# Attention and two feed-forward layers in one kernel: normalising twelve score tiles inside the product that turns them

## The chip, the cores and the metric

The kernel runs on one core of one Trainium2 chip. The metric is device time in microseconds (us), the median of several runs. A core has TensorE (PE, matrix products into PSUM; PEld is its weight load), VectorE (DVE), ScalarE (ACT), GpSimd (POOL) and SyncE (SP), each with its own in-order instruction queue. In the profile TensorE's clock is granted at one of two levels, 2.4 GHz (shown as 1.00) and 1.2 GHz (0.50).

## The reference, cut to what matters

```
q_rot, k_rot = rotate(q), rotate(k)                 # rotary embedding; q, k, v: (4, 8, 576, 64) float32
scores = q_rot @ k_rot.T / sqrt(64)
attn = exp(scores - max(scores))
attn = attn / (sum(attn) + 1e-09)                   # the step that the change moves
x = (attn @ v) as (2304, 512)
h = max(x @ w1, x @ w2, x @ w3)                     # 512 -> 768
y = h @ w_out                                       # 768 -> 512
g = y @ w_in; out = (g * sigmoid(g)) @ w_out2       # 512 -> 2048 -> 512
```

## The kernel before, in words

The attention works on 80 tiles, 20 for each of the 4 batches. A tile (b, hp, t) holds 128 query rows of the pair of heads hp, so its scores are two blocks of 128 x 576; the tile with t = 4 holds the last 64 queries of both heads on 128 partitions and has one block of 576. The list `tiles` takes, for each batch, first t = 0 and 1 of the four pairs and then t = 2, 3, 4 of the four pairs. Here tiles are counted from 0 in that order: tile 10 is the first with t = 4, and tiles[0:12] is tiles 0 to 11, all of batch 0.

Step j of `attention` (L625) does this for the tiles around j. `tile_scores` (L425) makes the scores of tile j on TensorE in float32 (L437 and L440, for t = 4 L430 and L431); there is one score buffer in PSUM. `tile_max` (L446) takes the row maximum on VectorE (L450) and the exponentials and their sums on ScalarE (L457, two instructions, one for each head). `tile_norm` (L463) runs for tile j-1: it adds 1e-9 to the sums on ScalarE (L466), takes the reciprocal on VectorE (L467), and scales the 128 x 576 exponentials of each head in place on ScalarE (L469). `tile_turn` (L532) runs for tile j-2 in batch 0: it transposes the tile in 9 pieces of 128 x 128 on TensorE (L551, three pieces for one PSUM buffer "tr", of which there are two) and copies each three out to the buffer `pt`, on ScalarE (L555) or VectorE (L557). A running count `evacs` chooses which: of the first 27 copies every third is on ScalarE, and later two of three (L554). A tile with t = 4 has six pieces (L540, L475, L476) and copies of its own. `av` (L559) then multiplies `pt` with v (L571, L575). The later batches turn their tiles by DMA and VectorE (`tile_move`, `tile_flip`) and are not touched.

Between these steps runs other work of the first 130 us. `qk_rope` and `qk_turn` (L387, L393, L399, L401 to L410) prepare q and k; GpSimd does most of the rotation. `prep_w1` loads the twelve pieces of w1, w2 and w3 as float64 and narrows each one: ScalarE L229, GpSimd L233 (for two pieces ScalarE L235), VectorE L248 and L249, a maximum on ScalarE (L155), and later a split in two float16 halves by GpSimd L175 and VectorE L178. From tile 8 on `moe1` (L674) adds groups of 12 or more float16 products (L670) for the first feed-forward layer, so many by a budget (`pace`, `RATE`), and these go on until the end of the kernel.

The order in which instructions stand in each engine's queue is made at build time by a scheduler; `tc.issue_after` pins a few of them. `z_p` is a ring of four 128 x 256 buffers, otherwise used when the second layer's weights are narrowed, which begins after step 20.

Of the kernel before, what the change touches and what calls it, by code (L numbers as in the profile page):

```python
# [17 lines left out]
P = 128  # L18
# [4 lines left out]
def fused_kernel(  # L23
# [439 lines left out]
    def tile_norm(key):  # L463
        e, m = e_t[key], heads(key)
        r = small.tile([P, 2], F32, tag="rec", name="rec")
        nc.scalar.activation(out=r[:, 0:m], in_=sum_t.pop(key)[:, 0:m], func=AF.Copy, bias=1e-9)  # L466
        nc.vector.reciprocal(out=r[:, 0:m], in_=r[:, 0:m])  # L467
        for g in range(m):
            nc.scalar.activation(out=e[:, HK[g]], in_=e[:, HK[g]], func=AF.Copy, scale=r[:, g:g + 1])  # L469

    def turn_last(e, to):

        tr = ps_t.tile([P, 512], F32, tag="tr", name="tr")
        with tc.issue_after(last["score"]):
            nc.tensor.transpose(tr[:, 0:P], e[:, 448:576], ident)  # L475
            nc.tensor.transpose(tr[0:64, P:2 * P], e[:, 512:576], ident)  # L476
        to = to.rearrange("p (i q) -> p i q", i=2)
# [54 lines left out]
    def tile_turn(key):  # L532
        b, hp, t = key
        n = P
        e = e_t.pop(key)
        pt, o = pt_of(key)
        if t == 4:
            tr = ps_t.tile([P, 512], F32, tag="tr", name="tr")
            for c in range(4):
                nc.tensor.transpose(tr[:, c * P:(c + 1) * P], e[:, c * P:(c + 1) * P], ident)  # L540
            t4 = tr.rearrange("p (c q i g) -> p g c i q", c=4, g=2, i=2)
            to = [pt[:, c:c + 4, o:o + 64].rearrange("p c (i q) -> p c i q", i=2) for c in (0, 5)]
            nc.scalar.activation(out=to[0], in_=t4[:, 0], func=AF.Copy)
            nc.vector.tensor_copy(out=to[1], in_=t4[:, 1])
            turn_last(e, pt[:, 4, o:o + 64])
            return
        for j in range(3):
            tr = ps_t.tile([P, 512], F32, tag="tr", name="tr")
            for i in range(3):
                c = 3 * j + i  # L550
                nc.tensor.transpose(tr[:, i * n:(i + 1) * n], e[0:n, c * P:(c + 1) * P], ident[0:n, 0:n])  # L551
            to, of = pt[:, 3 * j:3 * j + 3, o:o + n], tr[:, 0:3 * n].rearrange("p (a n) -> p a n", a=3)
            evacs[0] += 1
            if evacs[0] % 3 == 1 if evacs[0] < 28 else evacs[0] % 3:  # L554
                nc.scalar.activation(out=to, in_=of, func=AF.Copy)  # L555
# [65 lines left out]

    LOOSE = 25
    LAST = [(B - 1, hp, t) for hp in range(NP) for t in PARTS[1][2]]

# [821 lines left out]
```

## Time and profile before

| | us |
|---|---|
| median of 3 runs | 976.12 (973.97 to 977.35) |
| the profiled execution | 973.05, of which the span is 971.3 |
| TensorE busy in the span | 902.0 (93%) |
| VectorE, ScalarE, GpSimd busy | 710.9, 603.9, 442.3 |

The span runs from the first instruction to the last; 1.75 us lie around it. The page lists busy times of each engine over the span and groups of instructions by source line; the trace can be asked for any stretch of it. A row of a timeline gives the start, the length, the engine, the line, the operation and how many instructions it merges; an idle time before it stands in brackets with what ended it. Rows of TensorE overlap, since a product begins before the one ahead has ended: what one costs in a stream is the distance between two starts.

### The profile page before, as it was taken

Reading aid. Unit: us, or ns where it says so; the run is one execution under the profiler, and the core shown is the slowest. Engines: PE = TensorE matmul, PEld = TensorE weight load, DVE = VectorE, ACT = ScalarE, POOL = GpSimd, SP = SyncE. Lnnn points to the kernel's source line nnn. Section 1 sums busy time; section 2 is a strip of 40 time slices with the busy share of each in tenths; the row PEclk is TensorE's granted clock in tenths of the full one; section 3 lists DMA queues with packets and bytes.
Section 4 is the critical chain, followed back from the end, with each engine's and each line's share of the span. In section 5 each row is a group of like instructions: output and inputs, shape, how many; then the busy total and the mean of one; then the engine's idle time right before and its main releaser. Section 6 shows DMA issues by size and latency. Waiting matters only on the chain.

```text
span 971.3 us, 19058 instructions
## 1 busy us (share of the span) xinstructions
PE 902.0 (93%) x6802; PEld 667.4 (69%) x6802; DVE 710.9 (73%) x1295; ACT 603.9 (62%) x1381; POOL 442.3 (46%) x482
## 2 busy tenths in 40 slices
PE   2787898899999899999998999999998999999997
PEld 1454665566655566566654687788887888888886
DVE  6779888867789576898887667465787866856654
ACT  1987587757687666798877535363555545544442
POOL 6745584960325400421211047264486467365363
PEclk9788999999999999999999999999999999999999
DMA  6943034958888984899989763164553434324101
GB/s 153 295 135 108 17 109 125 185 108 187 196 184 192 202 153 87 229 237 244 264 234 208 175 206 126 51 210 130 162 167 99 134 122 136 123 91 136 61 1 44
DMA packets 185198, 146.29 MB, mean 151 GB/s; under 512 B 51216, under 2 KB 168720, under 8 KB 185104
## 3 DMA queue, kind: packets, MB, share of 16 engines
q1 hardware_dynamic: 183600, 144.36, 57.9%
q8 instruction: 54, 0.88, 0.4%
q10 hardware_dynamic: 1504, 0.72, 0.3%
q14 instruction: 40, 0.33, 0.1%
HBM read 90.51 MB, written 26.21 MB: 120 GB/s over the span
## 4 chain that ended last, share of the span: by engine, by line
PE 54%; DMA 10%; DVE 7%; ACT 6%; SPq 4%; issue 3%; POOL 2%; DVEq 0%; ACTq 0%; POOLq 0%
PE m L670 11%; PE m L1102 8%; PE mb L1102 6%; DMA pt<-e 4%; PE c L1165 4%; PE a L1165 4%; PE b L1165 4%; PE xp L575 3%; PE mg L670 3%; PE s L440 3%; ACT e L457 2%; PE d L1165 2%; SPq L508 2%; DMA w8s<-w8scr 2%; POOL gsum L1049 1%
## 5 line engine op out<-in xcount | busy, mean ns | idle before, releaser
L670 PEld LDWEIGHTS <-w 128*128 128x128 f16 x1632 | 160.3, 99 | 62.2 <-issue 18.1
L670 PE MATMUL m<-x,w 128*128 128x256 f16 (+1 forms) x1356 | 188.6, 289 | 10.7 <-DVE t L689 5.1
L1165 PEld LDWEIGHTS <-g 128*128 128x128 f16 x1485 | 145.2, 98 | 16.9
L1102 PEld LDWEIGHTS <-w8s 128*128 128x128 f16 x1344 | 131.0, 98 | 16.1 <-issue 0.9
L450 DVE TENSOR_REDUCE nb<-s 128x2 f32<-128x1152 f32 (+1 forms) x80 | 98.5, 1232 | 37.2 <-PE s L440 30.0
L457 ACT ACTIVATE e<-s,nb 128x576 f32<-128x576 f32 x144 | 105.1, 734 | 28.6 <-DVE nb L450 26.1
L469 ACT ACTIVATE e<-e,rec 128x576 f32<-128x576 f32 x144 | 104.0, 766 | 11.2 <-DVE rec L467 10.4
L366 POOL TENSOR_TENSOR w<-qk,sin_sb 128x512 f32<-128x512 f32 (+2 forms) x40 | 42.8, 1072 | 122.7 <-DMA qk<-in_q_dram 93.5
L575 PE MATMUL xp<-pt,vd 128*64 128x256 f32 (+1 forms) x512 | 79.0, 422 | 0.9 <-DVE pt L530 0.9
L440 PE MATMUL s<-T 64*128 64x512 f32 x256 | 78.7, 685 | 0.0
L970 POOL TENSOR_TENSOR zs<-za 128x128 f32<-128x128 f32 x32 | 16.5, 527 | 129.8 <-DMA za<-zwi 68.3
L530 DVE STREAM_TRANSPOSE pt<-pt 128x1024 f32<-128x1024 f32 (+1 forms) x60 | 67.6, 1127 | 9.4 <-DMA pt<-e 9.4
L1054 DVE SCALAR_TENSOR_TENSOR g<-gsum,sg,g 128x1024 f16<-128x1024 f32 x36 | 49.5, 1383 | 23.7 <-ACT g L1053 23.4
L1116 POOL TENSOR_TENSOR z<-t 128x256 f32<-128x256 f32 x32 | 27.1, 845 | 87.4 <-DVE t L1108 51.3
L1053 ACT ACTIVATE g<-gsum,sg 128x1024 f16<-128x1024 f32 x36 | 40.8, 1141 | 36.4 <-POOL gsum L1049 36.4
L670 PE MATMUL m<-h,wo 128*128 128x256 f16 (+1 forms) x448 | 62.1, 286 | 0.5 <-POOL wo L175 0.3
L575 PEld LDWEIGHTS xp<-pt,vd 128*64 128x64 f32 x512 | 35.6, 139 | 36.7 <-issue 15.7
L670 PEld LDWEIGHTS <-wo 128*128 128x128 f16 x512 | 49.5, 98 | 16.2 <-issue 2.5
L940 POOL TENSOR_TENSOR z<-z 128x256 f32<-128x256 f32 x32 | 29.6, 952 | 41.7 <-DMA z<-zwo 41.2
L1165 PE MATMUL b<-w,g 128*128 128x256 f16 x376 | 48.5, 273 | 0.0
L1165 PE MATMUL a<-w,g 128*128 128x256 f16 x376 | 47.9, 273 | 0.0
L1165 PE MATMUL c<-w,g 128*128 128x256 f16 x376 | 47.6, 273 | 0.0
(265 smaller groups left out, 1989.9 us busy)
## 6 DMA issues: line engine op xcount, KB each, us to landing
w8s<-w8scr SPq DMA_DIRECT2D x64, 448.0 KB, 4.2
pt<-e SPq DMA_DIRECT2D x192, 128.0 KB, 4.0
z<-in_moe_w_in_dram SPq DMA_DIRECT2D x32, 256.0 KB, 3.6
z<-in_moe_w_out_dram SPq DMA_DIRECT2D x32, 256.0 KB, 3.8
w8scr<-w8o SPq DMA_DIRECT2D x32, 256.0 KB, 3.7
w<-in_moe_w_dram SPq DMA_DIRECT2D x6, 768.0 KB, 5.2
wo<-in_moe_w_dram SPq DMA_DIRECT2D x6, 768.0 KB, 5.3
qk<-in_q_dram SPq DMA_DIRECT2D x32, 128.0 KB, 3.1
```

The lines of the kernel that those rows point to most:

```text
L366: tt(out=w4, in0=t4, in1=sin2, op=ALU.mult)
L440: last["s"] = last["score"] = nc.tensor.matmul(s[:, o:o + 512], qs[r], kt[r], start=True, stop=True).ins
L450: x = nc.vector.tensor_reduce(out=nb[:, 0:m], in_=both(s, 0, 960, 576) if m > 1 else s[:, 0:576], op=ALU.max, axis=AX.X, negate=True)
L457: x = nc.scalar.activation(out=e[:, HK[g]], in_=s[:, SK[g]], func=AF.Exp, bias=nb[:, g:g + 1], accum_out=sm[:, g:g + 1])
L469: nc.scalar.activation(out=e[:, HK[g]], in_=e[:, HK[g]], func=AF.Copy, scale=r[:, g:g + 1])
L530: nc.vector.transpose(out=x, in_=x)
L575: nc.tensor.matmul(xp[r, 0:n], v4[:, g, c, :], turned(c, g), start=False, stop=(c == 3))
L670: x = nc.tensor.matmul(ps[:, 0:n], l, r, start=(first and i == 0), stop=(not more and i == len(passes) - 1))
L1053: nc.scalar.activation(out=h, in_=x, func=AF.Copy, scale=sg_t[jb])
L1054: nc.vector.scalar_tensor_tensor(out=l, in0=x, scalar=sg_t[jb], in1=h, op0=ALU.mult, op1=ALU.subtract)
L1102: nc.tensor.matmul(o, l, r, start=(i == 0), stop=(i == len(passes) - 1))
L1165: x = nc.tensor.matmul(ps, l, r, start=first, stop=last_, skip_group_check=True)
```

## The change

For the twelve tiles of `DIAGONAL` the exponentials stay as they are. ScalarE instead writes a 128 x 128 diagonal matrix for each head, the identity scaled row by row with the reciprocals, into a buffer of the ring z_p (23 such matrices: two for eleven tiles and one for tile 10). The turn of a piece, which was a transpose against the identity, becomes a float32 product of the piece with that diagonal, so that it comes out both turned and normalised. The fifth piece of a two-head tile holds columns of both heads and is split into two products with 64 weight columns each, so such a tile has ten products in place of nine transposes. The rule for the copies out of "tr" becomes the same for all tiles, two of three on ScalarE: of the first 27 copies (tiles 0 to 8) 18 instead of 9 are on ScalarE, and 9 instead of 18 on VectorE.

```diff
--- before.py
+++ after.py
@@ -465,15 +465,26 @@
         r = small.tile([P, 2], F32, tag="rec", name="rec")
         nc.scalar.activation(out=r[:, 0:m], in_=sum_t.pop(key)[:, 0:m], func=AF.Copy, bias=1e-9)
         nc.vector.reciprocal(out=r[:, 0:m], in_=r[:, 0:m])
+        if key in DIAGONAL:
+            d = diag_t[key] = z_p.tile([P, 256], F32, tag="z", name="z")
+            for g in range(m):
+                nc.scalar.activation(out=d[:, g * P:(g + 1) * P], in_=ident, func=AF.Copy, scale=r[:, g:g + 1])
+            return
         for g in range(m):
             nc.scalar.activation(out=e[:, HK[g]], in_=e[:, HK[g]], func=AF.Copy, scale=r[:, g:g + 1])
 
-    def turn_last(e, to):
+    def turned(to, of, d):
+
+        if d is None:
+            return nc.tensor.transpose(to, of, ident)
+        return nc.tensor.matmul(to, of, d, start=True, stop=True)
+
+    def turn_last(e, to, d=None):
 
         tr = ps_t.tile([P, 512], F32, tag="tr", name="tr")
         with tc.issue_after(last["score"]):
-            nc.tensor.transpose(tr[:, 0:P], e[:, 448:576], ident)
-            nc.tensor.transpose(tr[0:64, P:2 * P], e[:, 512:576], ident)
+            turned(tr[:, 0:P], e[:, 448:576], d)
+            turned(tr[0:64, P:2 * P], e[:, 512:576], d)
         to = to.rearrange("p (i q) -> p i q", i=2)
         t4 = tr[:, 0:2 * P].rearrange("p (a q i g) -> p a g i q", a=2, g=2, i=2)
         nc.scalar.activation(out=to[0:64], in_=t4[0:64, 1, 0], func=AF.Copy)
@@ -534,24 +545,31 @@
         n = P
         e = e_t.pop(key)
         pt, o = pt_of(key)
+        d = diag_t.pop(key, None)
+        diag = lambda g: d if d is None else d[:, g * P:(g + 1) * P]
         if t == 4:
             tr = ps_t.tile([P, 512], F32, tag="tr", name="tr")
             for c in range(4):
-                nc.tensor.transpose(tr[:, c * P:(c + 1) * P], e[:, c * P:(c + 1) * P], ident)
+                turned(tr[:, c * P:(c + 1) * P], e[:, c * P:(c + 1) * P], diag(0))
             t4 = tr.rearrange("p (c q i g) -> p g c i q", c=4, g=2, i=2)
             to = [pt[:, c:c + 4, o:o + 64].rearrange("p c (i q) -> p c i q", i=2) for c in (0, 5)]
             nc.scalar.activation(out=to[0], in_=t4[:, 0], func=AF.Copy)
             nc.vector.tensor_copy(out=to[1], in_=t4[:, 1])
-            turn_last(e, pt[:, 4, o:o + 64])
+            turn_last(e, pt[:, 4, o:o + 64], diag(0))
             return
         for j in range(3):
             tr = ps_t.tile([P, 512], F32, tag="tr", name="tr")
             for i in range(3):
                 c = 3 * j + i
-                nc.tensor.transpose(tr[:, i * n:(i + 1) * n], e[0:n, c * P:(c + 1) * P], ident[0:n, 0:n])
+                to = tr[:, i * n:(i + 1) * n]
+                if c == 4 and d is not None:
+                    for g in range(2):
+                        turned(to[64 * g:64 * g + 64], e[:, c * P + 64 * g:c * P + 64 * g + 64], diag(g))
+                else:
+                    turned(to, e[:, c * P:(c + 1) * P], diag(c // 5))
             to, of = pt[:, 3 * j:3 * j + 3, o:o + n], tr[:, 0:3 * n].rearrange("p (a n) -> p a n", a=3)
             evacs[0] += 1
-            if evacs[0] % 3 == 1 if evacs[0] < 28 else evacs[0] % 3:
+            if evacs[0] % 3:
                 nc.scalar.activation(out=to, in_=of, func=AF.Copy)
             else:
                 nc.vector.tensor_copy(out=to, in_=of)
@@ -620,6 +638,7 @@
         at(u + 1, v_scale_b, b)
 
     LOOSE = 25
+    DIAGONAL, diag_t = tiles[0:12], {}
     LAST = [(B - 1, hp, t) for hp in range(NP) for t in PARTS[1][2]]
 
     def attention():
```

The scheduler moves instructions around these. The queues differ until the start of the second batch and stand in the same order from the score tile 26 on. Three places follow; names are those of the program (e exponentials, s scores, pt the turned tile, z the diagonal, w and wo weight pieces, T and tr buffers of the turns).

ScalarE from tile 1's exponentials (e_331) to tile 2's (e_352, in the changed kernel e_353). Before:

```order
L457 ACTIVATE e_331,sm_332<-s_325,nb_329 128x576 x2
L229 ACTIVATE w_0_141<-w_0_304 128x768
L466 ACTIVATE rec_356<-sm_332 128x2
L235 ACTIVATE w_0_304<-w_0_304 128x768
L469 ACTIVATE e_331<-e_331,rec_356 128x576 x2
L229 ACTIVATE w_0_141<-w_1_321 128x768
L155 ACTIVATE junk_409,w1m_139<-w_0_141 128x768
L229 ACTIVATE w_0_141<-wo_0_144 128x768
L393 ACTIVATE T_377<-tr_384 128x512
L457 ACTIVATE e_352,sm_353<-s_346,nb_350 128x576 x2
```

The same engine and place in the changed kernel:

```order
L457 ACTIVATE e_331,sm_332<-s_325,nb_329 128x576 x2
L573 ACTIVATE pt_363<-tr_364 128x3x128
L229 ACTIVATE w_0_141<-w_0_304 128x768
L466 ACTIVATE rec_357<-sm_332 128x2
L235 ACTIVATE w_0_304<-w_0_304 128x768
L573 ACTIVATE pt_363<-tr_369 128x3x128
L229 ACTIVATE w_0_141<-w_1_321 128x768
L471 ACTIVATE z_360<-ident_81,rec_357 128x128 x2
L155 ACTIVATE junk_412,w1m_139<-w_0_141 128x768
L229 ACTIVATE w_0_141<-wo_0_144 128x768 x2
L457 ACTIVATE e_353,sm_354<-s_347,nb_351 128x576 x2
```

The two scalings of 128 x 576 give way to two diagonals of 128 x 128; two copies to pt (L573, before L555) come in, one narrowing L229 is drawn ahead, and the copy L393 goes behind tile 2's exponentials.

TensorE from the end of tile 7's scores to the start of tile 8's (s_664, in the changed kernel s_677). Before:

```order
L551 MATMUL tr_628<-ident_81,e_536 128x128 x3
L551 MATMUL tr_692<-ident_81,e_572 128x128 x3
L122 MATMUL m_650<-ident_81,wm_0_648 1x128
L571 MATMUL xp_674<-pt_593,vd_0_131 128x256
L551 MATMUL tr_638<-ident_81,e_536 128x128 x3
L575 MATMUL xp_674<-pt_593,vd_0_131 64x256 x3
L130 MATMUL m_650<-amax_652,ones_82 128x1
L551 MATMUL tr_702<-ident_81,e_572 128x128 x3
L575 MATMUL xp_674<-pt_593,vd_0_131 64x256 x5
L551 MATMUL tr_697<-ident_81,e_572 128x128 x3
L437 MATMUL s_664<-kd_0_125,T_218 128x2x64
```

The same engine and place in the changed kernel:

```order
L480 MATMUL tr_706<-z_637,e_581 128x128 x3
L122 MATMUL m_663<-ident_81,wm_0_661 1x128
L480 MATMUL tr_640<-z_600,e_543 128x128 x3
L589 MATMUL xp_687<-pt_603,vd_0_131 128x256
L480 MATMUL tr_717<-z_637,e_581 128x128 x3
L130 MATMUL m_663<-amax_665,ones_82 128x1
L480 MATMUL tr_651<-z_600,e_543 128x128 x3
L593 MATMUL xp_687<-pt_603,vd_0_131 64x256 x3
L437 MATMUL s_677<-kd_0_125,T_218 128x2x64
```

The transposes L551 become products L480 with the diagonal z; five groups of three become four, and five of the eight products with v (L575, now L593) move behind tile 8's scores.

ScalarE between tile 10's exponentials and tile 11's (e_842, in the changed kernel e_861). Before:

```order
L229 ACTIVATE w_0_141<-wo_0_144 128x768
L469 ACTIVATE e_733<-e_733,rec_796 128x576 x2
L469 ACTIVATE e_781<-e_781,rec_846 128x576
L155 ACTIVATE junk_834,w1m_139<-w_0_141 128x768
L229 ACTIVATE wo_0_144<-w_0_937 128x512
L687 ACTIVATE t_952<-m_939 128x256
L155 ACTIVATE junk_877,w1m_139<-w_0_141 128x768
L555 ACTIVATE pt_801<-tr_850 128x3x128
L235 ACTIVATE w_0_937<-w_0_937 128x512
L229 ACTIVATE wo_0_144<-w_1_1035 128x512
L555 ACTIVATE pt_801<-tr_855 128x3x128
L457 ACTIVATE e_842,sm_843<-s_836,nb_840 128x576 x2
```

The same engine and place in the changed kernel:

```order
L229 ACTIVATE w_0_141<-wo_0_144 128x768
L573 ACTIVATE pt_819<-tr_825 128x3x128
L466 ACTIVATE rec_865<-sm_799 128x1
L155 ACTIVATE junk_853,w1m_139<-w_0_141 128x768
L573 ACTIVATE pt_819<-tr_875 128x3x128
L706 ACTIVATE t_974<-m_961 128x256
L229 ACTIVATE wo_0_144<-w_0_959 128x512
L155 ACTIVATE junk_898,w1m_139<-w_0_141 128x768
L471 ACTIVATE z_868<-ident_81,rec_865 128x128
L573 ACTIVATE pt_819<-tr_870 128x3x128
L235 ACTIVATE w_0_959<-w_0_959 128x512
L457 ACTIVATE e_861,sm_862<-s_855,nb_859 128x576 x2
```

Three scalings of 128 x 576 leave the queue and one diagonal comes in, with one copy to pt more; the second narrowing L229 of a wo piece goes behind tile 11's exponentials.

## Rows read from the trace of the kernel before

**Rows 1.** The page: span, and busy time of each engine with its instructions

```profile
span 971.3 us, 19058 instructions
PE 902.0 (93%) x6802; PEld 667.4 (69%) x6802; DVE 710.9 (73%) x1295; ACT 603.9 (62%) x1381; POOL 442.3 (46%) x482
```

**Rows 2.** Five stretches: length, busy time of each engine, TensorE clock, DMA share, GB/s

```profile
28.26:62.75 34.49, 26.52 (x116) 14.66 (x116) 28.88 (x48) 31.89 (x69) 20.84 (x14) 0.75 0.88 249
62.75:85.63 22.88, 19.75 (x119) 11.09 (x118) 19.05 (x39) 18.93 (x44) 10.25 (x7) 1.00 0.30 77
85.63:101.36 15.73, 11.15 (x49) 6.22 (x49) 14.04 (x23) 13.41 (x29) 7.79 (x5) 0.78 0.29 105
101.36:200.00 98.64, 90.16 (x619) 60.37 (x619) 79.32 (x146) 67.40 (x179) 72.73 (x69) 0.98 0.52 120
200.00:960.00 760.00, 737.79 (x5820) 564.40 (x5818) 549.28 (x1010) 464.02 (x1044) 309.76 (x352) 1.00 0.60 154
```

**Rows 3.** Groups by line and shape, whole span: busy us, mean ns of one

```profile
L469 ACT ACTIVATE e<-e,rec 128x576 f32<-128x576 f32 x144 | 104.0, 766 | 11.2 <-DVE rec L467 10.4
...
L557 DVE COPY pt<-tr 128x384 f32<-128x384 f32 x25 | 13.4, 547 | 1.9 <-PE tr L551 1.5
...
L520 ACT ACTIVATE pt<-tr 128x128 f32<-128x128 f32 x48 | 13.1, 272 | 15.5 <-PE tr L519 15.3
...
L555 ACT ACTIVATE pt<-tr 128x384 f32<-128x384 f32 x23 | 10.9, 482 | 1.5 <-PE tr L551 1.4
```

**Rows 4.** Timeline of ScalarE around the scaling of tile 1

```profile
32.31 1.40 ACT L469 ACTIVATE e<-e,rec 128x576 f32<-128x576 f32 x2
33.62 0.88 ACT L229 ACTIVATE w<-w 128x768 f32<-128x768 f32 x1
...
36.02 0.57 ACT L393 ACTIVATE T<-tr 128x512 f32<-128x512 f32 x1
36.49 0.71 ACT L457 ACTIVATE e<-s,nb 128x576 f32<-128x576 f32 x1
```

**Rows 5.** Timeline of TensorE at 2.4 GHz, in streams without a gap

```profile
107.56 0.82 PE L551 MATMUL tr<-ident,e 128*128 128x128 f32 x6
108.22 0.38 PE L670 MATMUL m<-x,w1f 128*128 128x256 f16 x2
...
111.17 0.39 PE L437 MATMUL s<-kd,T 128*128 128x128 f32 x2
111.49 1.13 PE L440 MATMUL s<-T 64*128 64x512 f32 x4
...
177.96 0.60 PE L571 MATMUL xp<-pt,vd 128*128 128x256 f32 x2
178.39 0.39 PE L437 MATMUL s<-kd,T 128*128 128x128 f32 x2
```

**Rows 6.** Three stretches, each within one level of the granted clock

```profile
55.70:62.60 6.90, 6.21 (x21) 3.44 (x21) 4.09 (x7) 5.10 (x12) 2.48 (x2) 0.51 0.83 201
62.60:86.40 23.80, 19.90 (x120) 11.09 (x118) 19.97 (x39) 19.85 (x46) 11.02 (x7) 1.00 0.32 86
86.50:89.90 3.40, 3.38 (x10) 1.48 (x11) 3.40 (x8) 1.95 (x4) 2.61 (x3) 0.51 0.59 238
```

**Rows 7.** Timeline of TensorE: the scores of tiles 6 and 7

```profile
57.66 2.08 PE L440 MATMUL s<-T 64*128 64x512 f32 x4
...
65.42 1.13 PE L440 MATMUL s<-T 64*128 64x512 f32 x4
```

**Rows 8.** Timeline of VectorE before tile 11's maximum

```profile
85.52 1.85 DVE L178 SCALAR_TENSOR_TENSOR w<-w,sw10s 128x768 f16<-128x768 f32 x1
...
92.99 1.34 DVE L450 TENSOR_REDUCE nb<-s 128x2 f32<-128x1152 f32 x1
```

**Rows 9.** Timeline of ScalarE before tile 11's exponentials

```profile
88.96 2.10 ACT L469 ACTIVATE e<-e,rec 128x576 f32<-128x576 f32 x3
...
96.25 0.75 ACT L457 ACTIVATE e<-s,nb 128x576 f32<-128x576 f32 x1
```

## Prediction, made before the changed kernel was run

> **What bounds the kernel now.** I read the busy times of the page first. The reader sees TensorE at 93% of the span, with VectorE and ScalarE some 190 and 300 us below it [rows 1]. A share over the whole span hides the stage that the change touches, so I cut the trace into stretches next, at the starts of the exponentials of tiles 1, 6, 10 and 12 [rows 2]. From 200 us to the end TensorE is busy for 737.79 of 760 us: that part is bound by TensorE, its instructions keep their order, and it can only move as a whole. From 101.36 to 200 us it is busy for 90.16 of 98.64. Before that it has room, and the three stretches have three different limits. From 28.26 to 62.75 us (tiles 1 to 6) ScalarE is the full engine, 31.89 of 34.49, TensorE has 26.52. From 62.75 to 85.63 (tiles 6 to 10) TensorE has 19.75 of 22.88, with VectorE and ScalarE near 19. From 85.63 to 101.36 (tiles 10 to 12) VectorE is the fullest, 14.04 of 15.73. All diagonals fall in these three stretches, but for the last pieces of tile 11. So the question is by how much tile 12 starts earlier or later; that shift is handed on to the end, since from there on the same work is left and TensorE is nearly full.
>
> I then read the granted clock [rows 6]. The stretch 62.6 to 86.4 us ran at 2.4 GHz, 55.7 to 62.6 and 86.5 to 89.9 at 1.2 GHz. What this costs is seen in one row of each level: the two score products of tile 6 took 2.08 us, those of tile 7 1.13 us [rows 7].
>
> **Price of one of each.** A pair of scalings goes: the next instruction starts 1.31 us after the pair (32.31 to 33.62) [rows 4]; a single one takes 0.77 us [rows 3]. The diagonal, 128 x 128 on ScalarE, isn't in the trace. From below, the nearest row is a plain copy of 128 x 128 with 0.272 us, from above a copy of 128 x 384 with 0.482 us [rows 3]. I take 0.30, as it is the 128 x 128 row that has the shape, and keep both ends: a pair then takes 0.60 (0.54 to 0.96), and a tile with two heads saves 0.71 us on ScalarE (0.35 to 0.77). A copy of a turned third costs 0.48 us on ScalarE and 0.55 us on VectorE [rows 3]; nine of them change engines.
>
> A turned piece costs 0.11 us in a stream: six of them take 107.56 to 108.22 [rows 5]. The product that replaces it isn't in the trace as a stream. The same shape once, followed by other scores, took 111.17 to 111.49, that is 0.32 us. A float32 product with the same 128 x 128 weights and twice the columns took 177.96 to 178.39, that is 0.43 us; half of it is 0.22 us. I take 0.22, since that row comes from a stream, and keep 0.32 as the upper end. The lower end is 0.11: the product feeds the same columns through the same weights and can't be cheaper than the transpose. Then a tile with two heads costs 10 x 0.22 - 9 x 0.11 = 1.2 us more TensorE, or 0.4 us for each group that fills one "tr" buffer. Eleven such tiles and six pieces of tile 10 come to 14 us (0 to 25), all at 2.4 GHz.
>
> The Trainium skill, "TensorE: Matmul & The Clock Gate", section "Terms", says that the transpose mode is four times as fast as a float32 product. By that rule the product would cost 4 x 0.11 = 0.44 us. This case's rows lie below it, with 0.22 for half of the double-width product and 0.32 for the single one; it has its place among the rivals.
>
> **The sum, stretch by stretch.** Each stretch is judged by its own limit.
>
> Tiles 1 to 6. Five tiles lose a pair of scalings, 5 x 0.71 = 3.6 us of ScalarE, and the queue gains five copies (nine stand there in the new order, four before), 5 x 0.48 = 2.4 us. That leaves 1.2 us for an engine that was full. Order adds and takes some of it: on the way to tile 2 one narrowing is drawn ahead and the copy L393 (36.02 to 36.49) goes behind the exponentials [rows 4], and on the way to tile 6 one narrowing fewer stands in front. VectorE loses the same five copies, 5 x 0.55 = 2.7 us out of 28.88. The maximum stands in VectorE's queue ahead of the exponentials, so part of that counts. I take -2.0 us. The lower end is -4 (both engines' savings count in full). The upper end is +3: TensorE gets 5 x 1.2 = 6 us more, 32.5 of 34.49 us, and would be the limit if the clock stays at 1.2 GHz for as long as now or the product costs 0.32.
>
> Tiles 6 to 10. Here the added products are in the way. Some 13 groups fall into the stretch, 13 x 0.4 = 5.2 us, and TensorE has 3.1 us idle [rows 2]. So 2.1 us remain if all idle time can be filled. Against this, the scheduler puts scores ahead of work that can wait. Between tile 7's and tile 8's scores the queue has four groups for five and three of the eight products with v for eight; VectorE loses four copies, 2.2 us, two of them in front of tile 9's maximum. I take +0.3 us, with -1 and +5.2 as ends.
>
> Tiles 10 to 12. Tile 11's exponentials start at 96.25 though its maximum was ready at 94.3 (92.99 and 1.34): ScalarE's queue stood between [rows 8, 9]. In front of them three scalings go (2.0 us, 88.96 to 90.96) and one narrowing of 0.6 us, and one diagonal and one copy come in, 0.8 us: 1.8 us less, as much as the gap. VectorE has one split L178 (1.85 us here) fewer between the two maxima [rows 8] and a short operation more. The products add about 8 groups, 3.2 us, into 4.6 us of idle TensorE. I take -2.0 us, ends -3 and +2.
>
> After tile 12. Two groups of tile 11 fall into a stretch without slack: 2 x 0.4 = +0.8 us. The first groups of the feed-forward layer stand up to 24 products later against the scores of tiles 13 to 19, and by tile 20 as many have been done as before; I cost that at nothing, since no product is added. What covers it is that TensorE is 91% busy there; if their weights come late, it costs the idle time it had anyway.
>
> New waits: a turned piece now waits for its diagonal instead of its scaled tile, and behind it in TensorE's queue stand the next scores. The diagonal is ready 0.7 us earlier in the chain than the scaling was, so I count no loss. The ring z_p is free until after step 20, so no diagonal waits for a buffer there. No DMA is added; the later loads keep their issuers and shift with the tiles.
>
> Sum: -2.0 + 0.3 - 2.0 + 0.8 = -2.9 us on an execution of 973.05 us (span 971.3), which makes 970.1. That execution lies 3.1 us under the median of the runs, so for a median I expect 976.1 - 2.9 = 973.2 us.
>
> **Rivals.** First, TensorE takes over (slower). The mechanism is in the queue of tiles 6 to 10: the products hold back the scores, since scores stand behind them in order. If none of the idle 3.1 us can be filled, that stretch costs 5.2; tiles 1 to 6 then gain nothing, as their scores are held up as well, tiles 10 to 12 gain 1 at most, and 0.8 follows. That is +5, 981 us. It decides from a product of about 0.27 us on, or when the clock stays at 1.2 GHz where it is now. For it speaks that TensorE would be at 32.5 of 34.49 us in the first stretch; against it that it had 8 us to spare there.
>
> Second, the clock stays up (much faster). The low stretches begin after idle or thin TensorE time in the first 100 us. With 14 us of products more there is less of it. The scores of four tiles (2, 3, 6 and 11) ran at 1.2 GHz; each would gain 0.95 us [rows 7] and some 0.25 in the product ahead of them: 4.8 us on top, 968.4 us. Against it: low stretches also begin where TensorE waits for ScalarE's queue, and those waits remain in part.
>
> Third, no change. The gain at tile 12 is lost between 101 and 200 us, where the weights' preparation on GpSimd and VectorE and the loads of the next weights set the pace and not the attention: 976 us. For it speaks that TensorE still has 8.5 us idle there [rows 2], so something else than TensorE ends last.
>
> Fourth, the product costs 0.44 us. A tile then takes 10 x 0.44 - 9 x 0.11 = 3.4 us more and a group 1.13: the first stretch needs 26.5 + 17 = 43.5 us of TensorE (+9), the second +14.7 - 3.1 = 11.6, the third 9 - 4.6 = 4.4, with 2.3 after it: +27 us, 1003 us. The row of 0.32 us speaks against it. This is the price by the rule of the Trainium skill named above.
>
> **How the numbers follow.** About 0.3% (2.9 us) is what a measurement of this kernel can tell from no change. My forecast has 0.46, with its own range 970 to 975.5; a little over half of that (0.25) lies beyond the bound, 0.21 within. The clock's rival has 0.17, no change 0.13, TensorE 0.21, the dear product 0.03. So faster 0.25 + 0.17 = 0.42, same 0.21 + 0.13 = 0.34, slower 0.24. The range 966.5 to 981 takes in the forecast, no change, most of the clock's case and about half of TensorE's; some 0.17 is left out.
>
> **What would show it.** The profile after should have 23 diagonals of 0.27 to 0.48 us. Its products L480 should stand 0.2 us apart in a stream; at 0.3 or more, TensorE has taken over. ScalarE from tile 1's exponentials to tile 6's should need about 2 us less, and tile 11's exponentials should start within 0.5 us of the end of its maximum. Tile 12's exponentials should start near 97.7 instead of 101.36 us. The prediction is wrong if that start is not earlier, if TensorE shows no idle time from tile 6 to tile 10 while ScalarE and VectorE do, or if tile 12 is early and the scores at 200 us are not.

## The result, and the profile after

The changed kernel takes 979.62 us (median of 7 runs, 977.34 to 982.75); the kernel before, run beside it, 973.07 us (7 runs, 971.17 to 977.35). The ratio is 1.0066 with a 95% interval of 1.0041 to 1.0091: slower by 6.5 us, where 2.9 us less was forecast. The time lies inside the range (966.5 to 981), the direction was wrong. The profiled execution took 979.45 us.

The page of the changed kernel, against [rows 1]: TensorE has 11 us more, ScalarE 4 us less, and the span is 6.2 us longer.

```profile
span 977.5 us, 19315 instructions
...
PE 913.0 (93%) x6929; PEld 680.6 (70%) x6929; DVE 710.8 (73%) x1286; ACT 599.8 (61%) x1390; POOL 444.5 (45%) x482
```

The stretches between the same landmarks as in [rows 2], the starts of the exponentials of tiles 1, 6, 10 and 12, here 28.16, 65.50, 92.44 and 108.00 (columns as there; the cut at 206.26 lies 6.26 us after the one at 200, and the last row runs to the end of the span, there to 960):

```profile
28.16:65.50 37.34, 27.71 (x160) 18.33 (x161) 25.44 (x41) 31.22 (x73) 22.95 (x15) 0.91 0.81 233
65.50:92.44 26.94, 26.27 (x169) 16.70 (x170) 20.24 (x38) 19.11 (x49) 9.89 (x7) 1.00 0.31 86
92.44:108.00 15.56, 12.44 (x74) 8.59 (x73) 13.03 (x21) 11.30 (x29) 7.59 (x5) 0.89 0.21 73
108.00:206.26 98.26, 89.97 (x602) 58.93 (x602) 79.73 (x145) 64.83 (x173) 72.48 (x68) 0.97 0.48 107
206.26:977.50 771.24, 745.67 (x5896) 571.71 (x5894) 555.12 (x1020) 467.22 (x1052) 311.51 (x353) 1.00 0.60 154
```

Tiles 1 to 6 take 37.34 us instead of 34.49, with ScalarE no longer full (31.22 of 37.34). Tiles 6 to 10 take 26.94 instead of 22.88, with TensorE busy for 26.27 of it. Tiles 10 to 12 take 15.56 instead of 15.73. Tile 12's exponentials start at 108.00; the forecast had 97.7, the kernel before 101.36. From there to the end 0.4 us is given back. Tile 11's exponentials were to start within 0.5 us of the end of its maximum: they start 2.4 us after it (98.81 and 1.33 against 102.57), and ScalarE, which was to be relieved there, waits 3.22 us for VectorE ahead of them. VectorE in the changed kernel, then ScalarE:

```profile
98.81 1.33 DVE L450 TENSOR_REDUCE nb<-s 128x2 f32<-128x1152 f32 x1
```

```profile
97.97 0.84 ACT L155 ACTIVATE junk<-w 128x768 bf16<-128x768 f32 x1 [3.22 <-DVE w L249]
...
102.57 0.75 ACT L457 ACTIVATE e<-s,nb 128x576 f32<-128x576 f32 x1
```

The groups of the new and the changed lines, against [rows 3] (busy us, mean ns of one, and the idle time ahead with what ended it):

```profile
L480 PE MATMUL tr<-z,e 128*128 128x128 f32 x186 | 33.5, 310 | 3.9 <-DVE kd L410 2.1 <-ACT pt L573 1.2 <-DVE pt L575 0.4
...
L573 ACT ACTIVATE pt<-tr 128x384 f32<-128x384 f32 x32 | 15.4, 490 | 8.4 <-PE tr L479 4.1 <-PE tr L480 4.1
...
L471 ACT ACTIVATE z<-ident,rec 128x128 f32<-128x128 f32 x23 | 8.0, 395 | 1.7 <-DVE rec L467 1.6
...
L480 PE MATMUL tr<-z,e 128*64 128x128 f32 x46 | 5.3, 298 | 0.0
```

The record of a diagonal is 0.395 us long (the bounds were 0.272 and 0.482). Records of ScalarE overlap, and where nothing is waited for, the next instruction starts 0.29 to 0.31 us after a diagonal's start (16 of the 23), which is the 0.30 that was taken. The 116 products have 232 records, two for each. ScalarE's 32 copies of turned thirds now wait 8.4 us for TensorE, 4.1 of it for products; before, 23 copies waited 1.5 us [rows 3].

How TensorE holds back the exponentials is seen at tile 6. TensorE from tile 5's scores to tile 6's in the kernel before, then in the changed kernel, and there VectorE and ScalarE:

```profile
49.86 0.49 PE L437 MATMUL s<-kd,T 128*128 128x128 f32 x2 [0.41 <-ACT e L457]
...
54.11 0.66 PE L387 MATMUL tr<-ident,qk 128*128 128x128 f32 x4 [1.71 <-DVE pt L557]
...
56.39 0.90 PE L551 MATMUL tr<-ident,e 128*128 128x128 f32 x3 [0.80 <-ACT T L393]
```

```profile
51.73 0.39 PE L437 MATMUL s<-kd,T 128*128 128x128 f32 x2
...
54.03 0.94 PE L480 MATMUL tr<-z,e 128*128 128x128 f32 x6 [0.60 <-ACT pt L573]
55.97 1.25 PE L480 MATMUL tr<-z,e 128*128 128x128 f32 x8 [1.00 <-DVE kd L410]
...
59.24 1.22 PE L589 MATMUL xp<-pt,vd 128*128 128x256 f32 x2 [1.58 <-ACT pt L573]
60.25 2.40 PE L480 MATMUL tr<-z,e 128*128 128x128 f32 x12
62.49 0.39 PE L437 MATMUL s<-kd,T 128*128 128x128 f32 x2
```

```profile
63.98 1.36 DVE L450 TENSOR_REDUCE nb<-s 128x2 f32<-128x1152 f32 x1 [4.97 <-PE s L440]
```

```profile
63.07 0.90 ACT L229 ACTIVATE w<-w 128x768 f32<-128x768 f32 x1
65.50 0.74 ACT L457 ACTIVATE e<-s,nb 128x576 f32<-128x576 f32 x1 [1.53 <-PE tr L480]
```

In the changed kernel TensorE waits 1.58 us for a copy by ScalarE, then makes six products in 2.24 us (0.37 each, part of them at 1.2 GHz), and only then the scores of tile 6, at 62.49 instead of 57.09, 5.4 us late. Tile 5's were 1.9 us late. Between the two, thirteen products stand for twelve transposes, and TensorE's waits come to 3.2 us instead of 2.5. The bracket at 65.50 names a product that the exponentials do not read; what they needed last is the maximum on VectorE, which ran from 63.98 to 65.34. The two engines wait for each other in turn.

### The profile page after: what moved, and what is told of

It is laid out like the page before. It is cut to its first block, busy times and chain, and to the rows that moved or that the text cites. A ratio compares the mean times of both kernels' runs of the same rounds, so it can differ in the third digit from the quotient of the medians.

```text
span 977.5 us, 19315 instructions
## 1 busy us (share of the span) xinstructions
PE 913.0 (93%) x6929; PEld 680.6 (70%) x6929; DVE 710.8 (73%) x1286; ACT 599.8 (61%) x1390; POOL 444.5 (45%) x482
## 4 chain that ended last, share of the span: by engine, by line
PE 58%; DVE 11%; DMA 10%; ACT 5%; issue 4%; SPq 4%; POOL 4%; DVEq 0%; ACTq 0%; POOLq 0%
PE m L689 12%; PE m L1121 8%; PE mb L1121 6%; DMA pt<-e 5%; PE c L1184 4%; PE xp L593 4%; PE a L1184 4%; PE b L1184 4%; PE s L440 3%; PE mg L689 3%; PE d L1184 2%; DVE nb L450 2%; SPq L519 2%; POOL gsum L1068 2%; ACT e L457 1%
## 5 line engine op out<-in xcount | busy, mean ns | idle before, releaser
L474 ACT ACTIVATE e<-e,rec 128x576 f32<-128x576 f32 x121 | 87.7, 766 | 9.6 <-DVE rec L467 9.1
L593 PE MATMUL xp<-pt,vd 128*64 128x256 f32 (+1 forms) x512 | 79.4, 420 | 0.6 <-DVE pt L541 0.6
L593 PEld LDWEIGHTS xp<-pt,vd 128*64 128x64 f32 x512 | 35.3, 138 | 36.3 <-issue 15.9
```

The source lines that it names most:

```text
L593: nc.tensor.matmul(xp[r, 0:n], v4[:, g, c, :], turned(c, g), start=False, stop=(c == 3))
```

## The experiments

Two theories were put against each other first: the products hold back the scores in TensorE's queue ("queue"), or the nine copies that went to ScalarE wait for TensorE and hold the exponentials ("copies"); a third was that the later tiles decide. All were timed in five rounds beside the kernel before; the ratio to it is given with its 95% interval. Each set has 6 to 12 executions of the run. One kernel was measured twice (g1 and g1b, below, on two chips), and its two ratios are 0.0030 apart. So a difference of under 0.3% between two ratios is not read, even where an interval is narrower.

**e1: the old copy rule.** Edit, against the changed kernel:

```diff
-            if evacs[0] % 3:
+            if evacs[0] % 3 == 1 if evacs[0] < 28 else evacs[0] % 3:
```

> The changed kernel with the old rule for who copies a turned third (diagonals and products stay; in the first nine such groups ScalarE takes about a third of the copies instead of two thirds). Theory 'queue': the products hold back the scores in TensorE's queue, whoever copies: it stays 5 to 8 us above the kernel before (978 to 981), tile 12's exponentials 5 to 8 us late. Theory 'copies': ScalarE's new copies wait for TensorE (8.2 us idle in front of them) and hold the exponentials: it falls back to 973 plus or minus 2, tile 12 within 2 us of before. Theory 'later part': tile 12 moves by less than 3 us and the end by some other amount, with no tie between the two.

Measured 980.26 us, 1.0085 (1.0052 to 1.0117); tile 12's exponentials are 5.1 us late. "Copies" falls.

**e2: the new copy rule alone**, the same edit backwards on the kernel before.

> The kernel before with the new copy rule alone (scalings and transposes as before). 'Queue': within -1 to +2 us of before, since TensorE gets nothing. 'Copies': +4 to +8 us, as in the changed kernel. 'Later part': any shift of tile 12 below 3 us, the end apart from it.

Measured 982.95 us, 1.0102 (1.0073 to 1.0132), tile 12 9.2 us late in an execution of 988.27 us, the longest of its six. With the scalings still on ScalarE the copies cost more than "copies" says, though TensorE got nothing. So both theories fit one run and miss one.

**e3: products alone**, against the identity, with the scalings kept and the old copy rule (shown in part; the diagonals of `tile_norm` are left out as well):

```diff
-        d = diag_t.pop(key, None)
+        d = ident if key in DIAGONAL else None
```

> The kernel before with each turned piece of the first twelve tiles as a float32 product with the identity (the scalings by ScalarE stay, the old copy rule, no diagonals). This is the added TensorE work alone. 'Queue': 12 us of TensorE (24 busy records' worth of products less transposes in the first 200 us) pass through: +8 to +14 us. 'Copies': 0 to +3, TensorE's idle 24 us take it in. 'Later part': +3 or less at tile 12, the end apart from it.

Measured 980.14 us, 1.0070 (1.0050 to 1.0090), tile 12 4.8 us late, tile 26 9.3 us. That is 6.8 us by the ratio, under what "queue" asks for and above "copies".

**e4: no scalings** in the first twelve tiles (in `tile_norm`, ahead of the scaling):

```diff
+        if key in tiles[0:12]:
+            return
```

> The kernel before without the normalisation of the first twelve tiles (their scalings are left out, nothing takes their place; the scale of v is made 1024 times smaller so that the sums stay in float16's range; the output is not the reference's). This is the relief of ScalarE alone, 23 x 0.66 = 15 us of it. 'Queue' and 'copies': tile 12's exponentials come 4 to 8 us earlier, and the end 3 to 6 us earlier. 'Later part': tile 12 comes earlier, but by 200 us the gain is lost, the end within 1.5 us of before.

Measured 975.99 us, 1.0036 (1.0015 to 1.0058). Work was only taken away, and the kernel did not get faster. Its tiles lead by up to 3.7 us at tile 18 and lag by 3.3 us at tile 20. No theory of added work explains that. Each of the four kernels had a new order as well: the scheduler draws the order of every engine from durations of its own, and these change with the edit.

So the next runs hold the order. At the end of the program, order-only edges are drawn on each engine and queue between neighbours in a given list, which is the kernel before's own order (or, in p2, that of e1):

```diff
+        for a, b in zip(chain, chain[1:]):
+            tc.add_manual_dep(b, a.name, m.DependencyInfo(m.DependencyClass.NoSync, m.DependencyReason.DATA), reason="order")
```

A diagonal takes the place of its scaling, a product that of its transpose. The kernel before with such edges and nothing else was not timed; g1 and g1b below, which have them, are not slower than before. The orders of before and e1 differ up to about tile 25; after that they are the same.

**p1: the work of e1 in the old order.**

> The arithmetic of the changed kernel with the old copy rule (diagonals, products; the same kernel as the run with the old copy rule, 980.3 us), but every engine's and queue's instructions are held in the order of the kernel before by order-only edges: each diagonal stands where its scaling stood, each product where its transpose stood. Theory 'work': the products' time on TensorE (12 us more busy in the first 206 us) costs, in whatever order: +5 to +8 us. Theory 'order': the new order, which the scheduler drew up from its own durations, costs: back to within 2 us of before, or below it by up to 3 us.

Measured 976.86 us, 1.0034 (1.0012 to 1.0056): 3.3 us, between the two.

**p2: the work of before in e1's order.**

> The arithmetic of the kernel before (scalings, transposes) held in the order of the changed kernel with the old copy rule. 'Work': within 2 us of before. 'Order': +4 to +9 us, with tile 12's exponentials 3 to 6 us late and the qk loads of tile 19's time late again.

Measured 978.73 us, 1.0053 (1.0028 to 1.0079). With the same work, the new order alone costs 5.1 us. (The profiled execution, 982.84 us, was the longest of its twelve.) Where it does in tile 19 is seen on TensorE, in the kernel before and then in p2:

```profile
139.77 1.13 PE L440 MATMUL s<-T 64*128 64x512 f32 x4
140.83 1.48 PE L670 MATMUL m<-x,w 128*128 128x256 f16 x12
142.15 0.27 PE L401 MATMUL tr<-ident,qk 128*128 128x128 f32 x1
...
145.87 1.12 PE L430 MATMUL s<-T,qd 128*128 128x512 f32 x2 [0.17 <-ACT e L457]
...
151.40 0.39 PE L437 MATMUL s<-kd,T 128*128 128x128 f32 x2
```

```profile
147.93 1.02 PE L430 MATMUL s<-T,qd 128*128 128x512 f32 x2
...
149.40 0.27 PE L401 MATMUL tr<-ident,qk 128*128 128x128 f32 x1
149.50 1.47 PE L670 MATMUL m<-x,w 128*128 128x256 f16 x12
152.54 0.66 PE L540 MATMUL tr<-ident,e 128*128 128x128 f32 x4 [1.57 <-ACT T L393]
154.01 0.30 PE L475 MATMUL tr<-ident,e 128*128 128x128 f32 x1 [0.81 <-DVE kd L410]
155.31 0.85 PE L551 MATMUL tr<-ident,e 128*128 128x128 f32 x3 [0.89 <-DVE pt L544]
155.96 0.63 PE L437 MATMUL s<-kd,T 128*128 128x128 f32 x2
```

Before, the turn of the next q and k (L401) stood ahead of tile 19's scores (L430), at 142.15. In p2 it stands behind them, so the copies out of it run when little else is left in front, and TensorE waits three times. From tile 19's to tile 20's scores it takes 8.03 us instead of 5.53. The changed kernel has the same: 7.91 us.

**p3: no scalings, old order.**

> The kernel before without the scalings of the first twelve tiles (left out: their normalisation), in the order of the kernel before otherwise. 15 us of ScalarE go and nothing is moved. 'Order': tile 12's exponentials 3 to 6 us earlier, and the end -2 to -5 us against before (in its own order it was +3.7). 'Work': the relief is worth nothing because ScalarE was not the limit: within 2 us of before.

Measured 970.64 us, 0.9976 (0.9955 to 0.9998): 2.3 us less by the ratio, under the 0.3% that is read. Tile 12's exponentials come only 0.6 us earlier, so "order" falls at tile 12. Here one sees what the relief of ScalarE turned into. ScalarE in p3, then the same instructions in the kernel before:

```profile
62.26 0.92 ACT L229 ACTIVATE w<-w 128x768 f32<-128x768 f32 x1 [3.24 <-DMA w<-in_moe_w_dram]
63.08 0.73 ACT L457 ACTIVATE e<-s,nb 128x576 f32<-128x576 f32 x1
...
89.65 0.84 ACT L155 ACTIVATE junk<-w 128x768 bf16<-128x768 f32 x1 [1.18 <-DVE w L249]
...
91.98 0.67 ACT L229 ACTIVATE wo<-w 128x512 f32<-128x512 f32 x1 [1.39 <-DVE w L249]
```

```profile
61.94 0.91 ACT L229 ACTIVATE w<-w 128x768 f32<-128x768 f32 x1 [1.80 <-DMA w<-in_moe_w_dram]
...
92.17 0.67 ACT L229 ACTIVATE wo<-w 128x512 f32<-128x512 f32 x1 [0.28 <-DVE w L249]
```

The relief does bring tile 5's exponentials forward, by 1.6 us. But ahead of tile 6's the narrowing L229 waits for its weights' load; without the scalings the wait is 3.24 us instead of 1.80, and the exponentials start at 63.08 instead of 62.75. Ahead of tile 11's it waits for VectorE: the 2.1 us of scalings [rows 9] became 1.18 and 1.39 us of waiting.

**p4: products alone, old order.**

> The kernel before with its turned pieces as products with the identity, scalings kept, in the order of the kernel before (in its own order it was +7.9). 'Order': +1 to +4, the part of 12 us of TensorE that its idle time does not take in. 'Work': +7 to +10 as in its own order.

Measured 979.07 us, 1.0064 (1.0039 to 1.0090): 6.2 us, the products cost in the old order too. p1, with diagonals for the scalings, is 0.30% below it, just what two samples of one kernel differ by; whether diagonals are worth anything beside the products stays open.

**h1 and h2: the halves of the new order**, cut at about tile 12, with the work of before.

> The arithmetic of the kernel before; every engine keeps the new order (that of the changed kernel with the old copy rule) up to about tile 12's exponentials and the old order from there on. Theory 'head': the new order costs where the change is made (tile 12's exponentials came 5.7 us late when the whole new order was used): tile 12 about +5.7, the end +3 to +6. Theory 'later': the head's delay is taken back by tile 18, as it was there (+0.6 us at tile 18), since the later stretch has idle time: the end within 1.5 us of before.

> The same with the halves exchanged: old order to about tile 12, the new order from there (GpSimd's rotations of the next batch stand behind one more weight's split, the loads of qk behind one of wo). 'Head': within 1.5 us of before. 'Later': tiles 19 to 25 late by 4 us or more against before, and the end +3 to +6.

Measured 977.73 us, 1.0054 (1.0023 to 1.0085), and 976.79 us, 1.0035 (1.0018 to 1.0053). Either half costs, the later one by little more than 0.3%; neither theory is right alone.

**s1 and s0: scores drawn ahead** (only TensorE's list is edited).

> The changed arithmetic in the old order (the run that took 1.0034 of before), with the scores of tiles 2, 4, 6 and 8 drawn ahead of the last turned groups that stand before them in TensorE's queue (4, 4, 6 and 9 instructions). If the products cost because they hold back the scores, tile 8's scores start up to 3 us earlier than 75.0 and the end loses at least half of its +3.3 us (within 1.7 us of before). If they cost as TensorE time wherever they stand, it stays at +3 to +4.

> The control: the kernel before with the same scores drawn ahead of its transposes. If the place of the scores is worth time by itself, it falls by about 1.5 us below before (tile 8's scores start 1.9 us after they could); if the old order is already right for it, within 1 us or slower.

Measured 980.94 us, 1.0082 (1.0059 to 1.0105), and 978.80 us, 1.0072 (1.0049 to 1.0095): both slower than with the scores left in place. The edit does not test its question. In s0 tile 2's scores start at 29.34 (29.97 before), but its maximum at 35.02 (33.56): VectorE's list was left as it was, and there the copies of the groups that were passed stand ahead of the maximum.

**n1: the changed kernel whole, old order**; only the nine copies had to be given a place.

> The changed kernel whole, with the new copy rule, in the order of the kernel before; the nine copies that change from VectorE to ScalarE stand in ScalarE's queue at the time at which VectorE made them before. If the order is what the change costs beyond the products, it stays near the run with the old copy rule in the old order: +1 to +5 us. If the copies on ScalarE cost by themselves (alone and in their own order they cost +9.9), +7 or more.

Measured 977.04 us, 1.0037 (1.0016 to 1.0058), against 1.0066 in its own order. The copies add nothing here, so e2's 9.9 us were theirs only together with its own order, or with the scalings that ScalarE still had there.

**d1 and d2: half of the tiles**, old order and old copy rule.

```diff
-    DIAGONAL, diag_t = tiles[0:12], {}
+    DIAGONAL, diag_t = tiles[0:6], {}
```

(d2 has `tiles[6:12]`.)

> Diagonals and products for tiles 0 to 5 only, old copy rule, order of the kernel before. The forecast put a gain of 2 us here (tiles 1 to 6, ScalarE full). If the relief of ScalarE is worth something where it is full: -2 to 0 us. If the products in front of the scores cost as elsewhere: +1 to +3, tile 6 late by about 1 us.

> The same for tiles 6 to 11 only. In tiles 6 to 8 TensorE has no idle time between two scores, so the products pass through: tile 8 late by 1.5 to 2 us, tile 12 by 1.5 to 2.5, the end +1.5 to +4. If the idle time of TensorE from tile 8 to tile 12 takes them in, as the forecast had it: within 1 us.

Measured 981.08 us, 1.0085 (1.0059 to 1.0111), and 980.37 us, 1.0072 (1.0046 to 1.0098). In d2's profile tile 8 and tile 12 are 2.2 us late, as the first of its two cases had it, but the end is 7.9 us late. Each half costs more than the whole (p1, 1.0034), which none had expected. The clock is one difference that the profiles show. The windows of a stretch in d1 and in p1 (the granted clock is the third figure from the right), and then in each the eight products ahead of tile 4's scores:

```profile
41.00:51.00 10.00, 9.78 (x39) 6.49 (x38) 6.24 (x15) 5.68 (x15) 4.18 (x3) 0.50 0.85 239
```

```profile
44.00:97.00 53.00, 47.41 (x313) 30.90 (x314) 43.32 (x78) 38.03 (x97) 23.73 (x14) 1.00 0.48 139
```

```profile
43.79 3.90 PE L480 MATMUL tr<-z,e 128*128 128x128 f32 x16
47.48 0.63 PE L437 MATMUL s<-kd,T 128*128 128x128 f32 x2
```

```profile
44.78 2.26 PE L480 MATMUL tr<-z,e 128*128 128x128 f32 x16 [0.18 <-DVE pt L575]
46.88 0.39 PE L437 MATMUL s<-kd,T 128*128 128x128 f32 x2
```

In d1 TensorE runs at 1.2 GHz from 41 to 51 us and the eight products take 3.69 us; in p1 it runs at 2.4 GHz from 44 to 97 us and they take 2.10. Tile 4's exponentials are 3.3 us late in d1 and 1.5 in p1. p4 (39.5 to 52.5 us) and d2 (36.0 to 49.7) have 1.2 GHz at that place too. The mean granted clock of every execution is known: its median is 0.982 in d1, 0.9855 in d2 and 0.9895 in p1. Within the five sets of the kernel before, 0.001 more of it goes with 0.3 to 0.5 us less time (a straight line through each set). By that, an estimate, the lower clock goes with about 3 of the 5.0 us between d1 and p1 and about 1.5 of the 3.7 between d2 and p1. Going together is not cause: the clock is a likely reason in d1, and it does not suffice in d2.

**g1, g1b and g2: half of the scalings on GpSimd.** Since p3's time was a little lower, the scaling of the second head of tiles 3 to 11 went to GpSimd, in the old order, measured twice; g2 is the same in its own order.

```diff
+            if g and key in tiles[3:12]:
+                nc.gpsimd.tensor_scalar(out=e[:, HK[g]], in0=e[:, HK[g]], scalar1=r[:, g:g + 1], scalar2=None, op0=ALU.mult)
+                continue
```

> The kernel before, in its own order, with the scaling of the second head of tiles 3 to 11 made by GpSimd (eight instructions; the first head's stays on ScalarE). TensorE gets nothing. If ScalarE's relief is worth time (half of the 2.3 us of the run without scalings): -1 us or a little more. If GpSimd is slower than 1.4 us for 128 x 576, the transposes wait for it: +1 to +4 us.

> The same kernel as the run with half of the scalings of tiles 3 to 11 on GpSimd in the order of the kernel before, once more. If its gain is real: 0.995 to 0.999 of before again, an interval under 1 with both samples. If it came from the one chip or the one set of runs: 1.000 or above. Its second profile shows whether tile 26 is late by 3 us again with an early end, or whether that lateness was that execution's.

> The same work in the order that the scheduler draws up for it. If a new order costs as it did for the other edits (+5 us between the two orders of one arithmetic): 1.002 to 1.007 of before. If GpSimd's help is worth it in any order: 0.995 to 0.999.

Measured 970.65 us, 0.9967 (0.9946 to 0.9988); the second time 972.74 us, 0.9997 (0.9978 to 1.0015); in its own order 976.53 us, 1.0026 (1.0005 to 1.0048). The first looked like a version that beats both kernels; the second did not bear it out. It beats the changed kernel and is not told apart from the one before. One such scaling takes GpSimd 1.77 us:

```profile
L470 POOL TENSOR_SCALAR e<-e,rec 128x576 f32<-128x576 f32 x8 | 14.1, 1767 | 4.2 <-DVE wm L263 2.6 <-DVE rec L467 1.2
```

The pairs of one work in two orders, as ratios to before:

| work | old order | own order |
|---|---|---|
| before | 1 | 1.0053 (p2, in e1's order) |
| changed, old copy rule | 1.0034 (p1) | 1.0085 (e1) |
| changed, whole | 1.0037 (n1) | 1.0066 |
| products only | 1.0064 (p4) | 1.0070 (e3) |
| no scalings | 0.9976 (p3) | 1.0036 (e4) |
| half on GpSimd | 0.9967, 0.9997 (g1, g1b) | 1.0026 (g2) |

## Why the prediction was wrong

By its own stretches, from the profiled executions (us against before; n1's landmarks are 28.89, 64.24, 89.15 and 104.65, its span 976.2):

| stretch | forecast | changed work, old order (n1) | changed kernel |
|---|---|---|---|
| ahead of tile 1 | 0 | +0.6 | -0.1 |
| tiles 1 to 6 | -2.0 | +0.9 | +2.9 |
| tiles 6 to 10 | +0.3 | +2.0 | +4.1 |
| tiles 10 to 12 | -2.0 | -0.2 | -0.2 |
| after tile 12 | +0.8 | +1.6 | -0.4 |
| sum | -2.9 | +4.9 | +6.2 |

The two profiles of one kernel (g1 and g1b) differ by 1.4 us in the stretch from tile 1 to tile 6 and by 3.8 us at tile 26, so smaller entries of single executions mean little by themselves.

**Tiles 1 to 6 and 10 to 12: the step "each stretch is judged by its own limit" failed.** It took the fullest engine, ScalarE, for the limit and counted its saving, less the copies. p3 shows that the whole saving, with nothing added, does not bring tile 6 forward and shortens tiles 10 to 12 by 0.4 us (15.31 from 85.44 to 100.75). A load and VectorE were due a moment later in ScalarE's queue; in the changed kernel the wait for VectorE is 3.22 us. The 0.28 us in front of L229 at 92.17 was there to be read: an engine that is full but already waits for another a little in front of the instruction that matters has no more to give than the slack of that other one. The forecast had -4.0 us for these two terms; n1 has +0.6 and the changed kernel +2.7.

**Tiles 6 to 10: the price was right, the place was not.** In the old order the queue between tile 7's and tile 8's scores has the same five turned groups as before and hardly a gap. The window of this stretch in the kernel before and in p1, and then TensorE's timeline of each:

```profile
66.48:72.17 5.69, 5.56 (x38) 3.60 (x37) 3.71 (x12) 4.90 (x12) 2.82 (x2) 1.00 0.14 54
```

```profile
67.55:75.03 7.48, 7.48 (x56) 5.64 (x54) 3.92 (x13) 4.64 (x12) 2.83 (x2) 1.00 0.02 7
```

```profile
66.48 0.88 PE L551 MATMUL tr<-ident,e 128*128 128x128 f32 x6
67.19 0.27 PE L122 MATMUL m<-ident,wm 128*1 128x128 f32 x1
...
72.17 0.39 PE L437 MATMUL s<-kd,T 128*128 128x128 f32 x2
```

```profile
67.55 1.60 PE L480 MATMUL tr<-z,e 128*128 128x128 f32 x12
68.99 0.27 PE L122 MATMUL m<-ident,wm 128*1 128x128 f32 x1
...
75.03 0.39 PE L437 MATMUL s<-kd,T 128*128 128x128 f32 x2
```

Six transposes take 0.71 us, six products 1.44: 0.24 us each where 0.22 was taken, and 0.37 more for a group where 0.4 was. The five groups add 1.79 us, all of it ahead of the scores. The forecast set 5.2 us of products against 3.1 us of idle TensorE in the whole stretch; the idle time lies elsewhere in it and took in none of these. This is the mechanism of the first rival, which had 981 us; but neither of the conditions set for it was met here, as the product was below 0.27 us and the clock at 2.4 GHz. In the changed kernel, where four groups stand there, tile 7's to tile 8's scores take 6.66 us (70.65 to 77.31), less than the 7.07 before. Its scores fall behind between tiles 5 and 6 (1.9, then 5.4 us late) and are 5.9 us late at tile 10. Of that, 2.65 us do not show in tile 6's exponentials: before, these stood in ScalarE's queue until 1.6 us after the end of their maximum (0.2 in the changed kernel), and the higher clock made the scores 1.2 us shorter. So much of the table's +4.1 for tiles 6 to 10 arose ahead of tile 6.

**The order was costed nearly at nothing, and it costs.** The forecast looked at the new order in a few places ahead of tile 12 and let the rest stand (of tiles 13 to 19: "I cost that at nothing, since no product is added"). p2, with not one product, is 5.1 us slower by e1's order, and its head (h1) and its later part (h2) each cost by themselves. Products cost too: 6.2 us in p4, 3.3 in p1 and 3.6 in n1, all in the old order. In the changed kernel about half of the loss up to tile 10 is work (n1) and half order, by the table above, which compares single executions. In the times the part of the order is 0.29% from n1 to the changed kernel, no more than two samples of one kernel differ by, and 0.51% from p1 to e1. So that an order costs is shown for e1's; how much of the changed kernel's 6.5 us is order is not.

**After tile 12.** The shift at tile 12 was to be handed on to the end. In the changed kernel it was (6.6 us at tile 12, 6.2 at the end), but by way of 14.3 us at tile 25, with the late turn at tile 19 in it. The reason given, that the later part is TensorE's and moves as a whole, holds only roughly: in g1's profile tile 26 is 2.95 us late and the end 1.9 us early.

**The second rival** had the clock stay up. It did: the mean granted clock is 0.986 instead of 0.978 in the profiles, its median over the executions 0.987, against 0.980 to 0.982 in the five sets of the kernel before. All seven kernels with products for all twelve tiles have a median of 0.986 or more, all with none 0.984 or less. Tile 6's scores ran at 2.4 GHz, from the first to the maximum's start 1.49 us instead of 2.69. By the estimate given with d1 this goes with 2 to 3 us, less than the 4.8 of the rival, and the delays took more: those scores started 5.4 us later.

**Sizes.** The product at 0.24 us speaks for the row of half a double-width product, not for 0.32. The Trainium skill's rule ("TensorE: Matmul & The Clock Gate", section "Terms": the transpose mode is four times as fast in float32; than what it does not say, and the forecast took a float32 product) gives an estimate of four times 0.12, that is 0.47; the trace at 2.4 GHz disagrees, the ratio is 2.0. At 1.2 GHz it was 0.46 (3.69 us for eight, in d1). On ScalarE the forecast mixed lengths of records with distances: a copy of a turned third has 0.48 us as a record, but the next instruction starts 0.37 to 0.39 us after its start where nothing is waited for (12 copies of the kernel before), so five copies are 1.9 us and not 2.4. That error ran against the saving and did not decide.

What stays open: why half of the tiles cost as much as all or more (d1, d2), beyond what goes with the clock; and how n1's 3.6 us divide between what the products cost and what the higher clock (0.989) gave back.

## What to carry to other kernels

When a scheduler draws the order from modelled durations, an edit is two changes: its work and a new order. Time the new work in the old order and the old work in the new one before you believe either; here even taking work away was slower until the order was held. The busiest engine of a stretch is worth only the slack up to the next wait in its own queue, so look at the small idle times just ahead of the instruction that matters; and time added on an in-order queue counts in full where the queue has no gap ahead of that instruction, however idle the engine is elsewhere.

## What the runs showed that was not expected

- A float32 product of 128 x 128 costs 0.24 us at 2.4 GHz and 0.46 at 1.2 GHz in a stream, and it leaves two records.
- A 128 x 128 copy with a scale from a tile has a record of 0.395 us on ScalarE, and the next instruction starts 0.30 us after its start; the plain copy from a "tr" buffer of that shape has a record of 0.272 [rows 3].
- Where products took the place of transposes in all twelve tiles, the mean granted clock was between 0.986 and 0.990 (medians of seven kernels); in the kernel before it was 0.980 to 0.982 (five sets).
- The scaling of 128 x 576 takes GpSimd 1.77 us and ScalarE 0.77.
- The same kernel, measured twice with twelve executions each on two chips, had 970.65 and 972.74 us, and 0.9967 and 0.9997 of the kernel before.
